# Causal scores in pieces of 64 queries by two experts, and paired half diagonal blocks, in a retention and soft-mixture attention kernel

## The chip, the cores and the metric

The kernel runs on one core of one Trainium2 chip. The metric is the device time of one execution in microseconds (us). TensorE (PE) does the matrix products and transposes, VectorE (DVE), ScalarE (ACT) and GpSimd (POOL) the elementwise work, and SyncE's queue (SP) issues the transfers.

## What is computed

Retention over 8 batches, 8 heads, 576 positions and head size 64 gives `x` of shape (8, 576, 512). On it works causal attention of four experts with head size 64, of which each token weighs the best two. All is float32.

```python
ret = scale * (q @ k.T) * Dmat            # Dmat: gamma ** (i - j) for i >= j, else 0
x = (ret @ v), heads joined               # 8 x 576 x 512
logits = x @ w_gate; best 2 of 4, softmax over them -> w
for e in range(4):
    q, k, v = x @ wq[e], x @ wk[e], x @ wv[e]
    scores = where(causal, -1e9, scale * (q @ k.T))
    a = softmax(scores)
    out += w[e] * ((a @ v) @ wo[e])
```

## The kernel before

Each batch has five chunks of queries, t = 0 to 4: four of 128 and a last one of 64. The 40 chunks go through a pipeline by steps `n`. A step does the retention of chunk `n` (`qk` L135, `old` L164, `own` L174, `st` L115), the attention scores of chunk `n - 6` (`scores`), the transposes of the chunk before it (`turn`), a piece of projections (`work`: q and k in `proj` L225, v in `vproj` L249, output in `outproj` L425), and last the product with the values of the chunk that was transposed (`values`, L400). The order on PE, DVE, ACT and POOL is the order in which the code records the instructions. So each engine works off its own list strictly in that order, and a step is named here by the chunk t whose scores it computes. A table `STEPS` says which piece of projections falls into which step; `end()` writes out the last steps by hand.

All PSUM tiles take turns on eight banks; a new tile waits until the tile eight before it has been read.

Scores (L315, L324): queries and keys of experts 2p and 2p + 1 lie in partitions 0 to 63 and 64 to 127 of pair tile p (index z says which half). Every product has 64 rows and 64 columns of the array. For t < 4 the 128 queries come in two halves i, each against all `w` = t0 + 128 keys. The loops p, i, z let four products in a row use four different quarters of the array. For t = 4 there are 64 queries and 576 keys in two parts j of 288, and output half and row half are both z:

```python
j = i ^ z
mm(ps[p][j][HALF[z]], q[p][HALF[z], l0:l0 + C], k[p][HALF[z], 288 * j:288 * j + 288], ...
```

A float32 product is two instructions on PE, and each has its own weight load.

The softmax takes each expert's scores with one DVE operation that adds the causal mask, negates and takes the extreme (L334; L338 for t = 4), and one ACT exponential with a running sum (L342). `normal` (L354 to L363) scales each expert's row by one over its sum times the gate weight, on DVE. `turn` (L378) transposes each expert's blocks of 128 keys on PE against the identity, up to four blocks in a bank, copied out by ACT (L383) for even experts and by DVE (L381) for odd ones. `values` multiplies with `vn` (L400): the two experts z of a pair stand in the two column halves of the array, all 128 keys of a block in its rows. The last block of t = 4 has only 64 keys and so 64 rows. `gate` (L276 to L292) makes the gate weights on DVE, after `vproj` of a range of chunks has copied out the logits (L254, L256).

Of the kernel before, what the change touches and what calls it, by code (L numbers as in the profile page):

```python
# [33 lines left out]
def kernel(ctx: ExitStack, tc: tile.TileContext, xf, xt, vkf, vkt,  # L34
# [200 lines left out]
    def vproj(b, r, t):  # L235
# [5 lines left out]
        if ti == 0:  # L241
            VN[b, r] = (sb.tile([128, nt, E * D], F32, name=f"vn{r}", bufs=2 - r),
                        sb.tile([128, nt, E], F32, name="lg", tag="lg"))
# [9 lines left out]
        act(vn[:C, ti], ps[:C, :E * D], AF.Copy)  # L253
# [14 lines left out]
    def gate(b, r):  # L268
# [22 lines left out]
        WT[b, r] = wt = sb.tile(sh2, F32, name="wt", tag="wt")  # L291
        v.tensor_mul(wt, ex, mx[:, 2].unsqueeze(2).to_broadcast(sh2))  # L292
# [5 lines left out]
    def scores(m):  # L298
# [6 lines left out]
        n = E if t < 4 else 2  # L305
        if t < 4:
            if t < 2:
                two = [bank([128, 2, w], "ss") for z in range(2)]
                ps = [two[e % 2][:, e // 2] for e in range(E)]
            else:  # L310
                ps = [bank([128, w], "ss") for e in range(E)]
            for p in range(2):
                for i in range(2):
                    for z in range(2):
                        mm(ps[2 * p + z][HALF[i]], q[p][HALF[z], l0 + 64 * i:l0 + 64 * i + 64], k[p][HALF[z], :w],  # L315
                           start=True, stop=True)
        else:
            ps = []
            for p in range(2):
                ps.append([bank([128, 288], "ss") for j in range(2)])  # L320
                for i in range(2):
                    for z in range(2):
                        j = i ^ z
                        mm(ps[p][j][HALF[z]], q[p][HALF[z], l0:l0 + C], k[p][HALF[z], 288 * j:288 * j + 288],  # L324
                           start=True, stop=True)
        p32 = sb.tile([128, n, w], F32, name="p32", tag="p32", bufs=2)
        sm = sb.tile([128, 2, E], F32, name="sm", tag="sm", bufs=3)
        nm = sb.tile([128, E], F32, name="nm", tag="nm", bufs=3)
        SS[m] = (p32, sm, n)

        def soft():
            for e in range(n):
                if t < 4:
                    v.tensor_tensor_reduce(p32[:, e], ps[e], mask[:, 512 - w:], -1.0, BIG, OP.add, OP.min, nm[:, e:e + 1])  # L334
                    bias = nm[:, e:e + 1]
                else:
                    for j in range(2):
                        v.tensor_tensor_reduce(p32[:, e, 288 * j:288 * j + 288], ps[e][j], mask4 if j else mask[:, :288],  # L338
# [3 lines left out]
                act(p32[:, e], p32[:, e], AF.Exp, bias=bias, scale=-1.0, accum_out=sm[:, 0, e:e + 1])  # L342
# [4 lines left out]
    def normal(m):  # L347
# [3 lines left out]
        p32, sm, n = SS[m]  # L351
# [4 lines left out]
        if t < 4:  # L356
            v.tensor_mul(rs, rs, wt[:, ti])
        else:
            for z in range(2):
                hr = slice(64 * z, 64 * z + 64)  # L360
                v.tensor_mul(rs[hr], rs[hr], wt[hr, ti, z::2])
        for e in range(n):
            v.tensor_scalar(p32[:, e], p32[:, e], rs[:, e:e + 1], None, op0=OP.mult)  # L363

    def turn(m):
        b, t = divmod(m, 5)
        p32, sm, n = SS.pop(m)
        nj = t + 1
        pth = sb.tile([128, n, nj, 128], F32, name="pth", tag="pth", bufs=2)
        PT[m] = pth  # L370
        for e in range(n):
            for j0 in range(0, nj, 4):
                js = range(j0, min(nj, j0 + 4))
                rows = slice(0, CH[js[0]][1])
                pt = bank([128, len(js), 128], "pt")
                for j in js:
                    c0, jw = CH[j]
                    nc.tensor.transpose(pt[rows, j - j0], p32[:, e, c0:c0 + jw], ident)  # L378
                o = pth[rows, e, j0:j0 + len(js)]
                if e % 2:  # L380
                    v.tensor_copy(o, pt[rows])  # L381
                else:
                    act(o, pt[rows], AF.Copy)  # L383
# [216 lines left out]
```

## Time and profile before

| what | value |
|---|---|
| median of 3 runs | 473.6 us (473.42 to 474.67) |
| span of the profiled execution | 471.3 us |
| PE busy | 453.0 us (96%) |
| PE weight loads busy | 400.0 us (85%) |
| DVE busy | 323.5 us (69%) |
| ACT busy | 259.5 us (55%) |
| POOL busy | 216.1 us (46%) |
| DMA | 50.98 MB, mean 108 GB/s |

The span goes from the first to the last instruction of the execution that was profiled; the page gives no other time of it, and the median is 2.3 us above the span. Busy times overlap between engines, and a float32 product counts as two instructions. A row of the timeline or of the groups counts a matmul until its result has landed, so that the last instruction of a row adds a fixed tail; differences between rows are free of it.

### The profile page before, as it was taken

How to read it: one execution, taken by the hardware profiler on the slowest of the kernel's cores; microseconds unless marked ns; L12 is line 12 of the kernel's file. 1: busy time of each engine (PE TensorE's matmuls, PEld its weight loads, DVE VectorE, ACT ScalarE, POOL GpSimd, SP SyncE). 2: the span in 40 equal slices, each digit the busy share in tenths (PEclk: the TensorE clock that was granted, in tenths of full speed). 3: DMA queues.
4: the chain of work that ended last, by engine and by line, in shares of the span. 5: the costliest groups of instructions: out<-in, count | busy, mean ns of one | idle time of the engine just before them, and what ended most of it. 6: DMA issues, size and time to landing. Idle time of an engine off the chain costs nothing.

```text
span 471.3 us, 19018 instructions
## 1 busy us (share of the span) xinstructions
PE 453.0 (96%) x7996; PEld 400.0 (85%) x7996; DVE 323.5 (69%) x1136; ACT 259.5 (55%) x814; POOL 216.1 (46%) x275
## 2 busy tenths in 40 slices
PE   7497999999999999999999999999999999999996
PEld 4496988899889898899988998899888998778885
DVE  2735788766797668976687658975679656882662
ACT  2653666555666456645564555654565555663472
POOL 1437464544564454654455445654546544511100
PEclk9589999999999999999999999999999999999999
DMA  7946223314261233314233143512423110010022
GB/s 288 381 142 219 91 93 116 113 46 147 92 217 56 84 134 110 137 47 144 96 131 108 39 143 106 210 50 92 146 92 136 48 58 3 2 47 1 2 79 78
DMA packets 22516, 50.98 MB, mean 108 GB/s; under 512 B 2720, under 2 KB 11680, under 8 KB 22432
## 3 DMA queue, kind: packets, MB, share of 16 engines
q1 hardware_dynamic: 22432, 49.77, 30.4%
q8 instruction: 63, 1.03, 1.0%
q14 instruction: 21, 0.17, 0.1%
HBM read 40.33 MB, written 9.44 MB: 106 GB/s over the span
## 4 chain that ended last, share of the span: by engine, by line
PE 89%; ACT 3%; DVE 3%; POOL 2%; DMA 2%; issue 1%; SPq 0%; ACTq 0%; POOLq 0%; DVEq 0%
PE pj L225 22%; PE ys L400 11%; PE po L425 11%; PE pv L249 11%; PE pt L378 10%; PE ss L315 8%; PE qk L135 4%; PE ss L324 3%; PE own L174 3%; PE st L115 3%; PE old L164 3%; DMA gi<-gi 2%; POOL x L184 1%; ACT gi L101 1%; DVE p L363 1%
## 5 line engine op out<-in xcount | busy, mean ns | idle before, releaser
L342 ACT ACTIVATE p<-p,nm 128x128 f32<-128x128 f32 (+4 forms) x144 | 83.1, 578 | 79.1 <-DVE nm L334 57.6
L186 POOL TENSOR_TENSOR xl<-x,xh 128x512 fp32r<-128x512 f32 (+1 forms) x38 | 45.3, 1192 | 96.5 <-ACT xh L185 96.5
L363 DVE TENSOR_SCALAR p<-p,sm 128x128 f32<-128x128 f32 (+4 forms) x144 | 78.7, 607 | 1.4
L414 POOL CAST yh<-y 128x256 fp32r<-128x256 f32 (+1 forms) x39 | 16.5, 424 | 113.6 <-ACT y L413 113.6
L334 DVE CUSTOM_DVE_ANT_0 p<-ss,mask 128x512 f32<-128x512 f32 (+3 forms) x128 | 56.4, 483 | 8.3 <-PE ss L315 7.9
L179 DVE TENSOR_TENSOR x<-x,own 128x256 f32<-128x256 f32 (+1 forms) x80 | 26.4, 364 | 51.2 <-ACT x L167 49.7
L378 PEld LDWEIGHTS pt<-con,p 128*128 128x128 f32 (+1 forms) x400 | 42.9, 139 | 20.2 <-issue 12.1
L141 POOL TENSOR_SCALAR_AFFINE_SELECT p<-p 64x512 f32<-64x512 f32 (+1 forms) x80 | 48.9, 611 | 23.3 <-ACT p L138 20.5
L400 PE MATMUL ys<-pth,vn 128*64 128x128 f32 (+2 forms) x960 | 56.6, 262 | 0.0
L378 PE MATMUL pt<-con,p 128*128 128x128 f32 (+1 forms) x400 | 52.9, 278 | 1.3 <-DVE nm L334 1.1
L400 PEld LDWEIGHTS ys<-pth,vn 128*64 128x64 f32 (+1 forms) x960 | 46.2, 136 | 8.1 <-issue 3.1
L184 POOL TENSOR_TENSOR x<-x,gi 128x512 f32<-128x512 f32 (+1 forms) x38 | 44.8, 1178 | 3.8 <-DVE x L179 0.5
L315 PE MATMUL ss<-k,q 64*64 64x512 f32 (+3 forms) x512 | 42.6, 432 | 0.0
L381 DVE COPY pth<-pt 128x512 f32<-128x512 f32 (+3 forms) x80 | 37.9, 485 | 4.8 <-PE pt L378 4.4
L102 POOL TENSOR_TENSOR vk<-vk,con 128x512 f32<-128x512 f32 (+1 forms) x34 | 33.9, 997 | 0.0
L383 ACT ACTIVATE pth<-pt 128x512 f32<-128x512 f32 (+3 forms) x80 | 33.1, 419 | 0.5 <-PE pt L378 0.4
L413 ACT ACTIVATE y<-ys 128x256 f32<-128x256 f32 (+1 forms) x39 | 14.1, 362 | 32.7 <-PE ys L400 32.3
L138 ACT ACTIVATE p<-qk 128x256 f32<-128x256 f32 (+1 forms) x80 | 24.6, 360 | 11.2 <-PE qk L135 11.2
L185 ACT ACTIVATE xh<-x 128x512 fp32r<-128x512 f32 (+1 forms) x40 | 23.2, 580 | 11.4 <-POOL x L184 7.2
L425 PE MATMUL po<-yh,who 128*128 128x320 f32 (+1 forms) x128 | 28.8, 306 | 0.6 <-ACT yh L409 0.6
L253 ACT ACTIVATE vn<-pv 128x256 f32<-128x256 f32 (+1 forms) x40 | 15.0, 380 | 24.9 <-PE pv L249 24.9
L225 PE MATMUL pj<-xh,whk 128*128 128x320 f32 (+1 forms) x128 | 24.2, 313 | 4.5 <-ACT xh L185 4.2
(89 smaller groups left out, 1022.6 us busy)
## 6 DMA issues: line engine op xcount, KB each, us to landing
x<-xf SPq DMA_DIRECT2D x32, 512.0 KB, 4.2
vk<-vkf SPq DMA_DIRECT2D x32, 512.0 KB, 5.3
out<-ot SPq DMA_DIRECT2D x32, 160.0 KB, 1.9
out<-ot SPq DMA_DIRECT2D x32, 128.0 KB, 1.8
raw<-wraw SPq DMA_DIRECT2D x4, 512.0 KB, 7.6
x<-xt SPq DMA_DIRECT2D x8, 256.0 KB, 2.7
vk<-vkt SPq DMA_DIRECT2D x8, 256.0 KB, 3.2
gi<-gi SPq DMA_DIRECT2D x1, 256.0 KB, 7.6
```

Source lines behind the costliest of these rows:

```text
L141: gp.affine_select(w, w, pattern=[[0, 4 * k], [1, 64]], base=0, channel_multiplier=-1, compare_op=OP.is_ge, fill=0.0)
L184: e.tensor_mul(x32, x32, gi[:, :, t0:t0 + C])
L186: e.tensor_sub(xl[:, :, l0:l0 + C], x32, f(xh[:, :, l0:l0 + C]))
L225: mm(ps, ww[:, kc, p * 128:(p + 1) * 128], xx[:, kc], start=(i == 0), stop=(i == 11))
L249: mm(ps[:C], xx[:, kc, l0:l0 + C], ww[:, kc], start=(i == 0), stop=(i == 11))
L315: mm(ps[2 * p + z][HALF[i]], q[p][HALF[z], l0 + 64 * i:l0 + 64 * i + 64], k[p][HALF[z], :w], start=True, stop=True)
L334: v.tensor_tensor_reduce(p32[:, e], ps[e], mask[:, 512 - w:], -1.0, BIG, OP.add, OP.min, nm[:, e:e + 1])
L342: act(p32[:, e], p32[:, e], AF.Exp, bias=bias, scale=-1.0, accum_out=sm[:, 0, e:e + 1])
L363: v.tensor_scalar(p32[:, e], p32[:, e], rs[:, e:e + 1], None, op0=OP.mult)
L378: nc.tensor.transpose(pt[rows, j - j0], p32[:, e, c0:c0 + jw], ident)
L400: mm(py[64 * z:64 * z + 64, p], VN[b, rr][0][jr, j - 2 * rr, e * D:(e + 1) * D], src, start=(j == 0), stop=(j == t))
L425: mm(ps, ww[:, p, d * 128:(d + 1) * 128], yy[:, p], start=(i == 0), stop=(i == 5))
```

## The change

For t < 4 a score piece now holds one half s of the chunk's queries (64) for the two experts z of each pair p: output half is p, tile is (s, z), and the first half ends at its own last key t0 + 64. `n` tiles e = 2s + z replace the four experts. For t = 4 the output half is p as well, and j is the outer loop. The mask is one triangle of 64 by 64 for all. The sums, weights and scalings follow this layout: `gate` writes its weights in four pieces (s, p), and `normal` puts the 64 diagonal keys of tile 1 behind those of tile 0. So one block of 128 holds the diagonal keys of the first query half for two experts z, and one transpose takes it. `turn` lists all blocks and puts four into a bank; ACT and DVE copy banks in turn. `values` reads the blocks of both query halves for j < t as one moving operand of two runs of 64, the full diagonal block of the second half by itself, and the paired diagonal block against `vd`, which holds the values of the chunk's first 64 keys for expert z in rows 64z to 64z + 63 and zeros in the other half. `vproj` writes `vd` with one more ACT and one more DVE copy, and the kernel clears it once at its start on POOL.

```diff
-    mask4 = const.tile([128, 288], F32, name="mask4")
-    gp.memset(mask[:, :384], 0.0)
-    gp.memset(mask4[:, :224], 0.0)
+    gp.memset(mask[:, :448], 0.0)
+    vd = [const.tile([128, 2, 2, D], F32, name=f"vd{t}") for t in range(5)]
+    for t in range(5):
+        for z in range(2):
+            gp.memset(vd[t][64 * (1 - z):64 * (1 - z) + 64, z], 0.0)
...
-        act(vn[:C, ti], ps[:C, :E * D], AF.Copy)
+        half = ps[:64, :E * D].rearrange("k (p z d) -> k p z d", p=2, z=2)
+        if t < 4:
+            act(vn[:, ti], ps[:, :E * D], AF.Copy)
+        act(vd[t][:64, 0], half[:, :, 0], AF.Copy)
+        v.tensor_copy(vd[t][64:, 1], half[:, :, 1])
...
-        v.tensor_mul(wt, ex, mx[:, 2].unsqueeze(2).to_broadcast(sh2))
+        for s in range(2):
+            ns = 2 if s else nt
+            for p in range(2):
+                v.tensor_mul(wt[HALF[p], :ns, s], ex[HALF[s], :ns, 2 * p:2 * p + 2],
+                             mx[HALF[s], 2, :ns].unsqueeze(2).to_broadcast([64, ns, 2]))
...
-            for p in range(2):
-                for i in range(2):
+            for s in range(2):
+                for p in range(2):
                     for z in range(2):
-                        mm(ps[2 * p + z][HALF[i]], q[p][HALF[z], l0 + 64 * i:l0 + 64 * i + 64], k[p][HALF[z], :w],
+                        e = 2 * s + z
+                        mm(ps[e][HALF[p]], q[p][HALF[z], l0 + 64 * s:l0 + 64 * s + 64], k[p][HALF[z], :ws[e]],
                            start=True, stop=True)
         else:
-            ps = []
-            for p in range(2):
-                ps.append([bank([128, 288], "ss") for j in range(2)])
-                for i in range(2):
+            ps = [[bank([128, 288], "ss") for j in range(2)] for z in range(2)]
+            for j in range(2):
+                for p in range(2):
                     for z in range(2):
-                        j = i ^ z
-                        mm(ps[p][j][HALF[z]], q[p][HALF[z], l0:l0 + C], k[p][HALF[z], 288 * j:288 * j + 288],
+                        mm(ps[z][j][HALF[p]], q[p][HALF[z], l0:l0 + C], k[p][HALF[z], 288 * j:288 * j + 288],
...
         for e in range(n):
-            v.tensor_scalar(p32[:, e], p32[:, e], rs[:, e:e + 1], None, op0=OP.mult)
+            parts = [(e, 0, ws[e])] if e != 1 else [(1, 0, t0)] * (t > 0) + [(0, t0 + 64, 64)]
+            for f_, c0, cw in parts:
+                i0 = c0 if f_ == e else t0
+                v.tensor_scalar(p32[:, f_, c0:c0 + cw], p32[:, e, i0:i0 + cw], rs[:, e:e + 1], None, op0=OP.mult)
...
+        blocks = [p32[:, z, 128 * j:128 * j + 128] for z in range(2) for j in range(t)] + [p32[:, 0, t0:t0 + 128]]
+        if t < 4:
+            blocks += [p32[:, 2 + z, 128 * j:128 * j + 128] for z in range(2) for j in range(t + 1)]
...
+            for j in range(t):
+                for z in range(2):
+                    a0 = z * t + j
+                    st = 2 * t + 1 + z
+                    src = pth[:, a0:a0 + st + 1:st, h] if t < 4 else pth[:, a0, h]
+                    e = 2 * p + z
+                    mm(py[HALF[z], p], VN[b, j // 2][0][:, j % 2, e * D:(e + 1) * D], src, start=(j == 0), stop=False)
+            if t < 4:
                 for z in range(2):
                     e = 2 * p + z
-                    src = pth[jr, e, j] if t < 4 else pth[jr, p, j, 64 * z:64 * z + 64]
-                    mm(py[64 * z:64 * z + 64, p], VN[b, rr][0][jr, j - 2 * rr, e * D:(e + 1) * D], src,
-                       start=(j == 0), stop=(j == t))
+                    mm(py[HALF[z], p, 64:], VN[b, r][0][:, t % 2, e * D:(e + 1) * D],
+                       pth[:, 2 * t + 1 + z * (t + 1) + t, h], start=(t == 0), stop=(t == 0))
+            for z in range(2):
+                mm(py[HALF[z], p, :64], vd[t][:, z, p], pth[:, 2 * t, h], start=(t == 0), stop=True)
```

Three places show how instructions move; a product is one row here. First, PE, scores of the first t = 4 chunk, before (`ss_1603` to `ss_1610` are the four banks, `k0` and `k1` the pairs p):

```order
L324 MATMUL ss_1603<-k0_381,q01_863 64x288
L324 MATMUL ss_1604<-k0_381,q01_863 64x288 x2
L324 MATMUL ss_1603<-k0_381,q01_863 64x288
L324 MATMUL ss_1609<-k1_382,q11_864 64x288
L324 MATMUL ss_1610<-k1_382,q11_864 64x288 x2
L324 MATMUL ss_1609<-k1_382,q11_864 64x288
```

and with the change:

```order
L334 MATMUL ss_1629<-k0_392,q01_881 64x288
L334 MATMUL ss_1631<-k0_392,q01_881 64x288
L334 MATMUL ss_1629<-k1_393,q11_882 64x288
L334 MATMUL ss_1631<-k1_393,q11_882 64x288
L334 MATMUL ss_1630<-k0_392,q01_881 64x288
L334 MATMUL ss_1632<-k0_392,q01_881 64x288
L334 MATMUL ss_1630<-k1_393,q11_882 64x288
L334 MATMUL ss_1632<-k1_393,q11_882 64x288
```

There are eight products as before, but four in a row now have four different pairs of row half (z, by bank) and column half (p).

Second, PE, the values of a t = 4 chunk, before (`vn_609` and `vn_1058` are the values of chunks 0 and 1 and of chunks 2 to 4):

```order
L400 MATMUL ys<-pth,vn_609 64x64 x4
L400 MATMUL ys<-pth,vn_1058 64x64 x6
L400 MATMUL ys<-pth,vn_609 64x64 x4
L400 MATMUL ys<-pth,vn_1058 64x64 x6
L135 MATMUL qk<-x 64x64 x16
```

and with the change, behind the values of t = 1 (its rows 1 to 6 took the place of eight products `ys<-pth,vn_609 64x128`):

```order
L411 MATMUL ys<-pth,vn_620 64x128 x2
L415 MATMUL ys<-pth,vn_620 64x64 x2
L418 MATMUL ys<-pth,vd_77 64x64 x2
L411 MATMUL ys<-pth,vn_620 64x128 x2
L415 MATMUL ys<-pth,vn_620 64x64 x2
L418 MATMUL ys<-pth,vd_77 64x64 x2
```

```order
L411 MATMUL ys<-pth,vn_620 64x64 x4
L411 MATMUL ys<-pth,vn_1070 64x64 x4
L418 MATMUL ys<-pth,vd_80 64x64 x2
L411 MATMUL ys<-pth,vn_620 64x64 x4
L411 MATMUL ys<-pth,vn_1070 64x64 x4
L418 MATMUL ys<-pth,vd_80 64x64 x2
```

The number of products is the same for t = 4, and all of them now have 128 rows; for t < 4 a pair of 128 columns became two pairs of 64.

Third, DVE, the end of the step of t = 1, before (`p` is the tile of scores, `sm` the sums, `lg` the logits):

```order
L357 TENSOR_TENSOR sm<-sm,wt 128x4
L363 TENSOR_SCALAR p_2054<-p_2054,sm 128x256 x4
L254 COPY lg<-pv 128x4 x2
L254 COPY lg<-pv 64x4
L256 COPY lg<-pv 64x4
```

and with the change:

```order
L368 TENSOR_TENSOR sm<-sm,wt 128x4
L373 TENSOR_SCALAR p_2087<-p_2087,sm 128x192
L373 TENSOR_SCALAR p_2087<-p_2087,sm 128x128
L373 TENSOR_SCALAR p_2087<-p_2087,sm 128x64
L373 TENSOR_SCALAR p_2087<-p_2087,sm 128x256 x2
L259 COPY vd_78<-pv 64x128
L260 COPY lg<-pv 128x4
L259 COPY vd_79<-pv 64x128
L260 COPY lg<-pv 128x4
L259 COPY vd_80<-pv 64x128
L260 COPY lg<-pv 64x4
L262 COPY lg<-pv 64x4
```

There are five scalings in the place of four, and a copy into `vd` ahead of each copy of logits.

## Rows read from the trace of the kernel before

**Rows 1.** The page: busy time by engine, and the ending chain by engine.
```profile
PE 453.0 (96%) x7996; PEld 400.0 (85%) x7996; DVE 323.5 (69%) x1136; ACT 259.5 (55%) x814; POOL 216.1 (46%) x275
...
PE 89%; ACT 3%; DVE 3%; POOL 2%; DMA 2%; issue 1%; SPq 0%; ACTq 0%; POOLq 0%; DVEq 0%
```
**Rows 2.** Busy time by stretch, start and one batch: length, busy us per engine, granted clock.
```profile
0.00:45.00 45.00, 32.66 (x818) 27.12 (x820) 19.50 (x53) 20.03 (x58) 19.64 (x28) 0.85 0.73 264
...
173.50:228.00 54.50, 54.50 (x1007) 49.04 (x1001) 39.86 (x140) 31.20 (x99) 27.96 (x36) 1.00 0.32 111
```
**Rows 3.** Groups by shape, PE, scores: busy us, mean ns, idle before.
```profile
L324 PE MATMUL ss<-k,q 64*64 64x288 f32 x128 | 17.5, 404 | 0.0
L315 PE MATMUL ss<-k,q 64*64 64x512 f32 x128 | 15.6, 591 | 0.0
...
L315 PE MATMUL ss<-k,q 64*64 64x384 f32 x128 | 12.7, 485 | 0.0
...
L315 PE MATMUL ss<-k,q 64*64 64x256 f32 x128 | 9.1, 379 | 0.0
...
L315 PE MATMUL ss<-k,q 64*64 64x128 f32 x128 | 5.2, 273 | 0.0
```
**Rows 4.** Timeline, PE, transposes of t = 1 and t = 2: start, us.
```profile
174.88 1.09 PE L378 MATMUL pt<-con,p 128*128 128x128 f32 x8
...
185.77 1.53 PE L378 MATMUL pt<-con,p 128*128 128x128 f32 x12
```
**Rows 5.** Timeline, PE, values of t = 1 and t = 2.
```profile
181.66 1.09 PE L400 MATMUL ys<-pth,vn 128*64 128x128 f32 x16
...
190.07 1.53 PE L400 MATMUL ys<-pth,vn 128*64 128x128 f32 x24
```
**Rows 6.** Timeline, PE, values of t = 4, windows of 0.3 and 0.6 us.
```profile
212.34 0.45 PE L400 MATMUL ys<-pth,vn 128*64 128x64 f32 x8
...
212.34 0.69 PE L400 MATMUL ys<-pth,vn 128*64 128x64 f32 x16
```
**Rows 7.** Chain, values of t = 4 and t = 0 up to the next `old`.
```profile
212.41 1.70 PE ys L400 x38
...
214.63 0.47 PE old L164 x31
...
225.53 0.59 PE ys L400 x8
...
226.74 0.47 PE old L164 x32
```
**Rows 8.** Timeline, from the scalings of t = 3 to its values.
```profile
189.74 3.63 DVE L363 TENSOR_SCALAR p<-p,sm 128x512 f32<-128x512 f32 x4
...
193.12 2.12 PE L324 MATMUL ss<-k,q 64*64 64x288 f32 x16
...
198.09 0.58 ACT L383 ACTIVATE pth<-pt 128x512 f32<-128x512 f32 x1
...
199.93 0.88 PE L400 MATMUL ys<-pth,vn 128*64 128x128 f32 x12
```
**Rows 9.** Groups by shape, DVE: a scaling, a small copy, the gate product.
```profile
L363 DVE TENSOR_SCALAR p<-p,sm 128x128 f32<-128x128 f32 x32 | 7.1, 286 | 0.3
...
L381 DVE COPY pth<-pt 64x128 f32<-64x128 f32 x8 | 2.2, 273 | 0.0
...
L292 DVE TENSOR_TENSOR wt<-ex,mx 128x12 f32<-128x12 f32 x8 | 1.4, 172 | 0.3
```
**Rows 10.** Timeline of the last steps.
```profile
445.88 1.67 DVE L363 TENSOR_SCALAR p<-p,sm 128x512 f32<-128x512 f32 x4
...
448.37 0.49 PE L378 MATMUL pt<-con,p 128*128 128x128 f32 x3
...
458.33 0.88 DVE L381 COPY pth<-pt 128x512 f32<-128x512 f32 x2 [3.81 <-PE pt L378]
458.44 1.82 PE L400 MATMUL ys<-pth,vn 128*64 128x64 f32 x40
```

More of the change, by code (lines that the diff above doesn't have):

```diff
@@ L350, in normal @@
         ti = t - RNG[r][2][0]
[L351 removed]
+        t0 = CH[t][0]
+        p32, sm, n, ws = SS[m]
         wt = WT[b, r]
@@ L355, in normal @@
         v.reciprocal(rs, sm[:, 0, :n])
[L356 to L361, printed above, removed]
+        v.tensor_mul(rs, rs, wt[:, ti].rearrange("p s z -> p (s z)") if t < 4 else wt[:, ti, 0])
         for e in range(n):
-            v.tensor_scalar(p32[:, e], p32[:, e], rs[:, e:e + 1], None, op0=OP.mult)
+            parts = [(e, 0, ws[e])] if e != 1 else [(1, 0, t0)] * (t > 0) + [(0, t0 + 64, 64)]
+            for f_, c0, cw in parts:
+                i0 = c0 if f_ == e else t0
+                v.tensor_scalar(p32[:, f_, c0:c0 + cw], p32[:, e, i0:i0 + cw], rs[:, e:e + 1], None, op0=OP.mult)
     def turn(m):
         b, t = divmod(m, 5)
-        p32, sm, n = SS.pop(m)
-        nj = t + 1
-        pth = sb.tile([128, n, nj, 128], F32, name="pth", tag="pth", bufs=2)
-        PT[m] = pth
[L371 to L383, printed above, removed]
-                yield
+        t0 = CH[t][0]
+        p32 = SS.pop(m)[0]
+        blocks = [p32[:, z, 128 * j:128 * j + 128] for z in range(2) for j in range(t)] + [p32[:, 0, t0:t0 + 128]]
+        if t < 4:
+            blocks += [p32[:, 2 + z, 128 * j:128 * j + 128] for z in range(2) for j in range(t + 1)]
+        pth = sb.tile([128, len(blocks), 128], F32, name="pth", tag="pth", bufs=2)
+        PT[m] = pth
+        for n, i0 in enumerate(range(0, len(blocks), 4)):
+            js = blocks[i0:i0 + 4]
+            pt = bank([128, len(js), 128], "pt")
+            for i, src in enumerate(js):
+                nc.tensor.transpose(pt[:, i], src, ident)
+            o = pth[:, i0:i0 + len(js)]
+            if n % 2:
+                v.tensor_copy(o, pt)
+            else:
+                act(o, pt, AF.Copy)
+            yield
     def values(m):
@@ L506 @@
             nc.sync.dma_start(rg, wraw[:, 4096:].rearrange("p (k w) -> p k w", k=4))
-            nc.sync.dma_start(mask[:, 384:], con_d[:, 220:])
-            for z in range(2):
-                nc.sync.dma_start(mask4[64 * z:64 * z + 64, 224:], con_d[:64, 220:284])
+            nc.sync.dma_start(mask[:, 448:], con_d[:, 220:])
         if n in (1, 4):
@@ L578, in _tables @@
     con[:, 200:220] = np.repeat(fac, 64, axis=0)
-    con[:, 220:348] = np.triu(np.full((128, 128), -1e9), 1)
+    con[:, 220:284] = np.tile(np.triu(np.full((64, 64), -1e9), 1), (2, 1))
     e = np.arange(E)
```

26 lines of the change are left out of this document (13 added, 13 removed).

## The prediction

> **What bounds the kernel now.** I read the page first. PE is busy 96% of the span, and the chain of work that ended last is 89% PE [rows 1], while DVE, the next, has 69%. Such shares are means, so I went on to the busy time by stretch: in one batch in the middle (54.5 us) PE is busy all of it, DVE 39.86 us, ACT 31.20 us, POOL 27.96 us, at full granted clock [rows 2]. PE works off its list without a gap there. So what PE's list loses in the six middle batches comes off the time, as long as the data that PE waits for come as much sooner. The first 45 us are another matter (PE busy 32.66 us, clock 0.85), but the change has no score piece in them, so I count nothing there. Then I took PE's groups by shape and its timeline for the price of each edit, and the rows of DVE and ACT around the one step where their work comes just in time.
>
> **The sum, on PE.** All times are set against the span of 471.3 us. The median is 473.6 us, 2.3 above it; I take that as what lies around the span and leave it.
>
> Scores of t = 4. Eight tiles, one a batch, took 17.5 us [rows 3], 2.19 us each. Before, only two quarters of the array are used (row half and column half are both z); now four are, as in the products of t < 4. Those cost 9.1 / 8 = 1.14 us for 256 keys and 12.7 / 8 = 1.59 us for 384 with the same eight products, so 288 keys come to 1.14 + 0.45 x 32/128 = 1.25 us. That saves 0.94 us a batch, 7.5 us in all.
>
> Scores of t < 4. From 128 to 512 keys the tile goes from 5.2 / 8 = 0.65 to 15.6 / 8 = 1.95 us [rows 3], 1.30 us for 384 columns in all eight products. Four of the eight lose 64 columns: 1.30 x 64/384 x 1/2 = 0.108 us, 32 times, 3.5 us.
>
> Transposes. Each tile has one less (4, 8, 12, 16, 10 become 3, 7, 11, 15, 9), 40 in all. Four more cost 1.53 - 1.09 = 0.44 us [rows 4], 0.11 us each: 4.4 us saved.
>
> Values of t < 4. Eight more instructions with 128 columns cost 0.44 us [rows 5], so a pair of experts (four instructions) 0.22 us. With 64 columns eight cost 0.69 - 0.45 = 0.24 us [rows 6], a pair 0.12 us. For each tile and p one pair at 0.22 becomes two at 0.12: +0.02, 64 times, 1.3 us more.
>
> Values of t = 4. The pairs with only 64 rows go. From the last end before the values to the start of the next `old` the chain has 214.63 - 212.41 = 2.22 us; for t = 0, where all pairs have 128 rows, 226.74 - 225.53 = 1.21 us with two pairs of 0.22 [rows 7]. Ten pairs of 0.12 in their place make 1.21 - 0.44 + 1.20 = 1.97 us. That saves 0.25 us, 2.0 us in all.
>
> Sum: -7.5 - 3.5 - 4.4 + 1.3 - 2.0 = -16.1 us.
>
> **What is given back.** DVE gets more instructions. Each batch has five copies into `vd` (0.27 us by the nearest copy), four more scalings (0.29 us for the nearest, 128 wide) and six more gate products (0.17 us) [rows 9]: at most 3.5 us, without the score and copy columns that fall away. That makes 43.4 us at most in a batch of 52.5 us, no new bound on the whole. ACT's five copies into `vd`, of which one takes the place of `vn`'s, have the idle 23 us of its batch. The ten clearings on POOL come ahead of its first selection, which waits for the first products of the retention; were they not covered there, they would delay only the first chunk. The mask's one transfer in the place of three frees SP; nothing on the path waits for it.
>
> The place to watch is the step of t = 4. The values of t = 3 start at 199.93, and the last ACT copy of their blocks ends at 198.09 + 0.58 = 198.67 [rows 8]: 1.26 us to spare. PE gains ahead of it, since the scores of t = 3: 0.11 there, 0.11 in the transposes of t = 2, 0.94 in the scores of t = 4 and 0.11 in those transposes, less 0.04 in the values of t = 2: 1.23 us. The copy is at the end of a chain on DVE and ACT that PE's gain does not pull forward: the four scalings of t = 3 take 3.63 us, 0.9 each for 512 columns [rows 8], though the four in the last steps take 1.67 us [rows 10]; POOL works beside the former. Five scalings of 1920 columns in all stand in place of four of 2048. The fifth costs between nothing (fewer columns make up for it) and 0.9 us (a slow one). I take 0.15 us a batch, near the lower end because 128 columns fewer save 0.2 us at that rate; over seven batches 1.0 us.
>
> The last steps give back more. Before the transposes of the last t = 3 tile the scalings end at 445.88 + 1.67 = 447.55, and PE starts at 448.37 [rows 10], 0.82 us to spare. Those scalings wait for the gate, which now has a copy into `vd` (0.27) and three more products (0.5) ahead of it, and for one more scaling. So the 0.94 us that PE gains in the scores just before is waited out: 0.9 us back. For the last t = 4 tile the values now need both experts' banks at once; before, the first matmul started at 458.44 while DVE's copies went on until 459.21 [rows 10], 0.77 us later. A transpose less and one copy fewer soften this: 0.5 us back.
>
> -16.1 + 1.0 + 1.4 = -13.7 us: 473.6 - 13.7 = **459.9 us**, or a span of 457.6.
>
> **The rivals.**
>
> *The step of t = 4 turns to DVE's bound.* If each fifth scaling costs 0.9 us, the slow rate above, all of it lies on PE from the second batch on, for there is no room left (1.26 against 1.23). In place of 0.15 us that is 0.9 us a batch, 5.3 us more: 465.2 us. For it: the slow rate is there in this very step, four times in a row. Against: the columns get fewer. Chance 0.14.
>
> *The change doesn't do what it says for t = 4:* four quarters don't run beside each other there. Then 7.5 us of the sum are gone: 467.4 us. Against: the products of t < 4 have the same four quarters in the same order and run at 1.14 us for 256 keys. Chance 0.04.
>
> *Weight loads show.* The new products in `values` are short, and each instruction brings a load of 64 columns. If these loads did not hide, the 256 added instructions (960 become 1216) would cost half a transpose with its load of 128 columns each, 0.055 us: 14.1 us, 474.0 us, no change. The row speaks against it: with 64 columns eight instructions take 0.24 us [rows 6], 0.03 each, less than 0.055, so their loads already run beside the products. The Trainium skill, "TensorE: Matmul & The Clock Gate", Part 3 under "What overlaps and what doesn't", says that a weight load runs beside a matmul in flight only where the row groups differ, and in `values` all products use all rows; by that rule this rival would be the likeliest. The trace disagrees with it, as the 0.24 us show. Chance 0.03.
>
> *Slower: the moving operand in two runs.* For j < t the values read two blocks of 64 columns that lie apart, by one instruction. No row shows that shape; the nearest are single runs of 64 and 128 columns, 0.12 and 0.22 us a pair [rows 5, 6]. Below, it costs nothing; above, if each run were read as long as a full one, 0.22 us more for each of 12 pairs a batch, 2.64 us, 21.1 us in all: 481.0 us. It decides from 13.7 / 96 = 0.14 us a pair. I take nothing, since the columns are the same. Chance 0.03.
>
> **How the numbers follow.** The forecast with its own spread (give-backs of 0 to 5 us) has 0.76, the rivals 0.14, 0.04, 0.03 and 0.03. Nothing given back makes 457.5; a little below that, for price rows that round, is the lower end, 456.8. The upper end takes in most of DVE's rival: 465.0. About 0.15 is left out. A measurement of this kernel can tell about 0.3%, 1.4 us, from no change. Faster by over that: the forecast and the first two rivals, 0.94; within it, the weight loads, 0.03; slower, the two runs, 0.03.
>
> **What would show it.** Right: on PE, t = 4 scores fall from 2.19 to about 1.25 us a tile with the same instruction count, 360 transposes stay, 64-column pairs in `values` stay at 0.12 us, and a middle batch takes 52.5 to 53 us. DVE's rival: idle time ahead of the values of t = 3, with ACT's or DVE's copy of the blocks as the releaser. Two runs: `values` rows of t = 1 to 3 that grow by more than 0.04 us a tile. Weight loads: pairs of 64 columns well over 0.12 us. The last steps: a wait ahead of the transposes of the last t = 3 tile, with DVE's scalings as the releaser. Wrong altogether would be a middle batch of 54 us or more with no group of PE's longer: then a wait that I have not seen took the gain.

## The result and the profile after

| | before | after |
|---|---|---|
| median | 473.51 us (472.54 to 474.67, 4 runs) | 468.81 us (467.65 to 469.49, 4 runs) |
| ratio | | 0.9899 [0.9878, 0.992] |
| span of the profiled execution | 471.3 us | 467.1 us |

The change gains 4.7 us where 13.7 were forecast, and the time lies above the range's upper end of 465.0. The page of the changed kernel, first the busy times, then the ending chain, then the queue that carries PE's instructions (number of packets, MB, share of 16 engines); the first two answer to [rows 1]:

```profile
PE 445.1 (95%) x8212; PEld 397.8 (85%) x8212; DVE 335.7 (72%) x1208; ACT 260.8 (56%) x830; POOL 219.5 (47%) x284
...
q8 instruction: 65, 1.06, 0.9%
...
PE 73%; DVE 12%; ACT 9%; issue 2%; DMA 2%; POOL 1%; SPq 0%; DVEq 0%; ACTq 0%; POOLq 0%
```

PE's busy time fell by 7.9 us, the span by 4.2 alone. The chain says where to look: DVE and ACT, 3% each before, now hold 21% of it. The groups by shape on PE (busy us, mean ns, idle before), to be laid beside [rows 3]:

```profile
L388 PE MATMUL pt<-con,p 128*128 128x128 f32 x360 | 48.7, 279 | 1.5 <-DVE nm L349 1.1 <-DVE p L373 0.2
L411 PE MATMUL ys<-pth,vn 128*64 128x128 f32 x384 | 33.4, 280 | 1.6 <-ACT pth L393 1.6
...
L334 PE MATMUL ss<-k,q 64*64 64x288 f32 x128 | 10.0, 406 | 0.7 <-DVE lg L260 0.7
```

The t = 4 scores went from 17.5 to 10.0 us, 1.25 a tile, just as forecast. But they now have 0.7 us of idle time before them, and the values 1.6 us, with ACT's copies of the blocks as the releaser. Where PE stands still is told by the busy time by stretch. I divided both traces where the first projection product of a t = 0 or t = 2 step starts. Before (length, busy us of PE, PEld, DVE, ACT, POOL, granted clock, DMA share, GB/s):

```profile
45.20:65.90 20.70, 20.29 (x395) 18.29 (x392) 17.07 (x68) 11.77 (x39) 12.49 (x14) 1.00 0.30 95
...
175.70:230.30 54.60, 54.60 (x1002) 49.10 (x1000) 39.89 (x141) 31.20 (x100) 28.06 (x36) 1.00 0.32 110
...
424.80:471.30 46.50, 42.49 (x410) 35.78 (x410) 21.23 (x78) 20.98 (x61) 4.82 (x10) 1.00 0.12 41
```

and after:

```profile
45.70:69.40 23.70, 21.70 (x401) 18.88 (x399) 19.34 (x75) 12.67 (x44) 12.44 (x14) 0.93 0.33 105
...
176.90:230.10 53.20, 53.00 (x1027) 48.49 (x1026) 41.45 (x150) 31.19 (x102) 28.31 (x36) 1.00 0.33 113
...
420.30:467.10 46.80, 40.99 (x440) 34.97 (x439) 22.64 (x90) 22.62 (x66) 5.32 (x11) 1.00 0.13 46
```

With the dividing points to the hundredth, the differences are:

| stretch | before | after | difference |
|---|---|---|---|
| to the first batch's t = 0 projections | 45.21 | 45.67 | +0.46 |
| on to its t = 2 projections | 20.71 | 23.70 | +2.99 |
| six batches, to the last one's t = 2 | 327.99 | 322.25 | -5.74 |
| on to its t = 0 (the last steps' order) | 30.93 | 28.65 | -2.28 |
| on to the end | 46.45 | 46.80 | +0.35 |

The forecast's 1.86 us a batch (16.1 / 8 less 0.15) would be -11.2 for the six batches. So two things have to be explained: 5.4 us in the six batches, and 3 us lost at once in the first batch, where I had looked for no loss (by the sum that stretch should have won 0.4 us). The start's 0.46 us is less than the changed kernel's runs below differ there among themselves (44.34 to 46.30), and the last two stretches come to 1.9 us where the forecast has 2.1.

**The first batch.** Timeline of the changed kernel from the t = 1 scalings (start, us):

```profile
59.79 3.63 DVE L373 TENSOR_SCALAR p<-p,sm 128x192 f32<-128x192 f32 x5
...
63.44 0.28 DVE L259 COPY vd<-pv 64x128 f32<-64x128 f32 x1
63.73 0.16 DVE L260 COPY lg<-pv 128x4 f32<-128x4 f32 x1
...
64.04 0.33 PE L176 MATMUL own<-p,vk 64*64 64x64 f32 x4 [1.77 <-POOL p L143]
...
64.53 0.68 PE L176 MATMUL own<-p,vk 64*64 64x64 f32 x28 [0.16 <-DVE lg L260]
...
66.17 2.55 PE L327 MATMUL ss<-k,q 64*64 64x320 f32 x16
```

The same place before:

```profile
59.29 3.10 DVE L363 TENSOR_SCALAR p<-p,sm 128x256 f32<-128x256 f32 x4
...
62.31 0.28 DVE L254 COPY lg<-pv 128x4 f32<-128x4 f32 x3
...
62.60 0.75 PE L174 MATMUL own<-p,vk 64*64 64x64 f32 x30 [0.41 <-DVE lg L254]
```

The `own` products need a bank that holds value projections (`pv`), and DVE frees it by its copies, which stand behind the scalings of t = 1. Before, three copies of logits took 0.28 us together; now a `vd` copy goes ahead of each, and the scalings are five. PE stands for 1.77 us instead of 0.41. (The row names POOL's selection as releaser. It isn't that: in a run below the same products start before it. PE goes on 0.15 us after the first `lg` copy, 63.73 + 0.16 us, and stands again until the second.) Other batches have the output projections in this step as cover, the first has none yet. In this execution, behind the wait, the granted clock falls to the lower of its two levels, 1.2 GHz; windows of 1 us of the changed kernel:

```profile
63.00:64.00 1.00, 0.00 (x0) 0.00 (x0) 0.94 (x4) 0.06 (x1) 0.94 (x2) 1.00 0.62 127
...
66.00:67.00 1.00, 1.00 (x24) 0.72 (x23) 0.57 (x4) 0.00 (x0) 0.80 (x1) 0.50 0.71 139
67.00:68.00 1.00, 1.00 (x12) 0.27 (x4) 0.79 (x5) 0.00 (x0) 0.46 (x1) 0.50 0.94 356
```

PE did nothing from 63 to 64; from 66 to 68 the clock is 0.50.

**The step of t = 4.** Timeline after, the rows that answer to [rows 8]:

```profile
190.81 4.21 DVE L373 TENSOR_SCALAR p<-p,sm 128x448 f32<-128x448 f32 x5
...
194.10 1.15 PE L334 MATMUL ss<-k,q 64*64 64x288 f32 x16
...
199.90 0.58 ACT L393 ACTIVATE pth<-pt 128x512 f32<-128x512 f32 x1
...
199.93 0.43 PE L411 MATMUL ys<-pth,vn 128*64 128x128 f32 x2
...
200.53 0.76 PE L411 MATMUL ys<-pth,vn 128*64 128x128 f32 x9 [0.17 <-ACT pth L393]
```

Before, the last ACT copy ended 198.67 - 189.74 = 8.93 us after the start of the t = 3 scalings; now 200.48 - 190.81 = 9.67. Of the 0.74 us more, the scalings are 0.58 (4.21 against 3.63). PE starts the values of t = 3, does two instructions, and stands until 200.53. They take 2.53 us up to the next `qk` where they took 1.90.

**The last steps.** Timeline after, to be laid beside [rows 10]:

```profile
441.23 1.74 DVE L373 TENSOR_SCALAR p<-p,sm 128x448 f32<-128x448 f32 x5
...
443.40 2.27 PE L388 MATMUL pt<-con,p 128*128 128x128 f32 x15 [1.09 <-DVE nm L349]
...
454.50 0.62 PE L411 MATMUL ys<-pth,vn 128*64 128x64 f32 x13 [0.21 <-DVE pth L391]
...
457.77 0.68 PE L411 MATMUL ys<-pth,vn 128*64 128x128 f32 x8 [0.55 <-ACT pth L393]
```

### The profile page after: what moved, and what is told of

It is laid out like the page before. It is cut to its first block, busy times and chain, and to the rows that moved or that the text cites. A ratio compares the mean times of both kernels' runs of the same rounds, so it can differ in the third digit from the quotient of the medians.

```text
span 467.1 us, 19651 instructions
## 1 busy us (share of the span) xinstructions
PE 445.1 (95%) x8212; PEld 397.8 (85%) x8212; DVE 335.7 (72%) x1208; ACT 260.8 (56%) x830; POOL 219.5 (47%) x284
## 3 DMA queue, kind: packets, MB, share of 16 engines
q8 instruction: 65, 1.06, 0.9%
## 4 chain that ended last, share of the span: by engine, by line
PE 73%; DVE 12%; ACT 9%; issue 2%; DMA 2%; POOL 1%; SPq 0%; DVEq 0%; ACTq 0%; POOLq 0%
PE pj L227 22%; PE po L442 10%; PE pv L251 7%; PE ss L327 7%; PE ys L411 7%; PE pt L388 6%; PE qk L137 4%; PE own L176 3%; DVE p L349 3%; DVE p L373 2%; PE st L117 2%; PE old L166 2%; ACT p L353 2%; PE ys L418 2%; DMA gi<-gi 2%
## 5 line engine op out<-in xcount | busy, mean ns | idle before, releaser
L353 ACT ACTIVATE p<-p,nm 128x64 f32<-128x64 f32 (+6 forms) x144 | 79.6, 554 | 86.0 <-DVE nm L344 57.8
L373 DVE TENSOR_SCALAR p<-p,sm 128x64 f32<-128x64 f32 (+8 forms) x176 | 88.3, 566 | 1.4
L388 PEld LDWEIGHTS pt<-con,p 128*128 128x128 f32 x360 | 38.7, 141 | 21.5 <-issue 10.2
L344 DVE CUSTOM_DVE_ANT_0 p<-ss,mask 128x128 f32<-128x128 f32 (+7 forms) x128 | 52.3, 452 | 6.2 <-PE ss L327 6.1
L388 PE MATMUL pt<-con,p 128*128 128x128 f32 x360 | 48.7, 279 | 1.5 <-DVE nm L349 1.1
L411 PE MATMUL ys<-pth,vn 128*64 128x128 f32 (+1 forms) x640 | 43.9, 258 | 1.9 <-ACT pth L393 1.6
L327 PE MATMUL ss<-k,q 64*64 64x448 f32 (+7 forms) x512 | 42.1, 416 | 0.6 <-issue 0.6
L411 PEld LDWEIGHTS ys<-pth,vn 128*64 128x64 f32 x640 | 31.3, 137 | 8.5 <-ACT pth L393 3.6
L393 ACT ACTIVATE pth<-pt 128x512 f32<-128x512 f32 (+1 forms) x64 | 32.6, 514 | 0.6 <-PE pt L388 0.3
L176 PE MATMUL own<-p,vk 64*64 64x64 f32 x1152 | 28.9, 226 | 3.3 <-POOL p L143 1.8
L187 ACT ACTIVATE xh<-x 128x512 fp32r<-128x512 f32 (+1 forms) x40 | 23.1, 578 | 11.2 <-POOL x L186 7.1
```

Of the source, the lines that this page charges most:

```text
L176: mm(own[r][HALF[u], g, i], vk[HALF[r], s, 0, 2 * g + u], p[HALF[r], g, s, u], start=True, stop=True)
L327: mm(ps[e][HALF[p]], q[p][HALF[z], l0 + 64 * s:l0 + 64 * s + 64], k[p][HALF[z], :ws[e]], start=True, stop=True)
L344: v.tensor_tensor_reduce(p32[:, e, :ws[e]], ps[e], mask[:, 512 - ws[e]:], -1.0, BIG, OP.add, OP.min, nm[:, e:e + 1])
L353: act(p32[:, e, :ws[e]], p32[:, e, :ws[e]], AF.Exp, bias=bias, scale=-1.0, accum_out=sm[:, 0, e:e + 1])
L373: v.tensor_scalar(p32[:, f_, c0:c0 + cw], p32[:, e, i0:i0 + cw], rs[:, e:e + 1], None, op0=OP.mult)
L388: nc.tensor.transpose(pt[:, i], src, ident)
```

## The experiments

Theory A was that PE's gain is real and is waited out behind DVE: at the values of t = 3 in every batch, and at the banks in the first.

**One part undone: the quarters.** The t = 4 scores in an order that names only two quarters of the array in its first four products and the other two in the rest:

```diff
-            for j in range(2):
-                for p in range(2):
-                    for z in range(2):
+            for d in range(2):
+                for j in range(2):
+                    for z in range(2):
+                        p = z ^ d
```

> Edit: the changed kernel with the t = 4 score products recorded so that only two quarters of the array lie side by side (z, then p = z xor d), eight products as before. Theory A (the gain of the t = 4 scores is mostly waited out, since the values of t = 3 wait for a chain on DVE and ACT): the t = 4 scores go from 1.25 back to about 2.2 us a tile by the rows, PE's list grows by 0.9 us a batch, but the wait of 0.6 us ahead of the values of t = 3 goes; net +0.3 us a batch in seven, so about 470 to 472 us against 468.8. Rival B (that wait has nothing to do with the scores' gain, each microsecond on PE's list counts): +0.9 a batch, 7 us in all, about 476 us.

468.45 us, ratio 0.9907 [0.9888, 0.9927]. The edit did not do what it was made for. The group of the scores:

```profile
L335 PE MATMUL ss<-k,q 64*64 64x288 f32 x128 | 11.6, 410 | 0.7 <-DVE lg L260 0.7
```

11.6 us instead of 10.0, far from the 17.5 of two quarters [rows 3], so it says nothing about A or B.

**The scores twice.** A cleaner way to take PE's gain back: the same products, issued once more.

```diff
-            for j in range(2):
+            for j in [0, 1, 0, 1]:
```

> The changed kernel with every score product of the t=4 step issued twice into the same banks (the same products, so nothing is left out). It puts back about 1.05 us of TensorE work a batch where the change took 0.9 us out. Theory A (most of what the scores gave there is waited out later in the same step, at the t=3 values, behind the fifth scaling and ScalarE's copy): the wait of 0.57 us there shrinks to nothing, so the time rises by the rest alone, 0.4 to 0.6 us a batch, 3 to 5 us in all: 472 to 474 us. Rival B (TensorE bounds the step from end to end, and the missing gain lies elsewhere): the whole 1.05 us a batch shows, 8 to 9 us in all: 477 to 478 us, and the t=3 values still wait.

471.67 us, ratio 0.9961 [0.9946, 0.9976], 2.9 us above the change. Its timeline:

```profile
192.54 2.12 PE L334 MATMUL ss<-k,q 64*64 64x288 f32 x32
...
199.25 0.88 PE L411 MATMUL ys<-pth,vn 128*64 128x128 f32 x12
```

The scores have grown by 2.12 - 1.15 = 0.97 us, and the values run without a stand. A middle batch takes 53.6 us, against 53.2 with the change. So of 0.97 us a batch 0.4 shows; the rest had been waited out. This decides for A in its place, the step of t = 4. The median is a little under A's 472 to 474; the first batch's clock stays full in this trace (more of that below).

**One scaling fewer on DVE.** For t = 3 the two halves of the diagonal block are brought together by products with the identity, not by a fifth scaling:

```diff
-            parts = [(e, 0, ws[e])] if e != 1 else ...
+            parts = [(e, 0, ws[e])] if e != 1 or t == 3 else ...
...
+                if src is None:
+                    for z in range(2):
+                        mm(pt[HALF[z], i], p32[:, z, t0:t0 + 64], ident, start=True, stop=True)
```

> Edit: the changed kernel; for t = 3 alone the scaling of tile 1 is one instruction again, the diagonal keys stay where they are, and two float32 products against the identity (one per column half, two instructions each) put their transposes into the paired block. PE's list grows by about 0.11 us a batch, DVE's chain of t = 3 loses the fifth scaling. Theory A: the scalings of t = 3 end about 0.5 us sooner after their start, the wait ahead of the values of t = 3 falls from about 0.6 to 0.1 us, net -0.4 us a batch, about 466 us. Rival B (the fifth scaling is hidden; the wait is ACT's own order of copies): the wait stays, +0.1 us a batch, about 469.5 us.

468.16 us, 0.9893 [0.9873, 0.9913]: the change's time, where A had about 466 us. The four scalings take 3.57 us and the stand at the values is gone (1.93 us), as A had it, but with these products the transposes took 2.02 us instead of 1.61, 0.41 more where I had counted 0.11. What was won on one side was mostly paid on the other: a middle batch takes 53.0 us.

**The last scaling of t = 3 on ACT.**

```diff
+                if t == 3 and e == 3:
+                    act(p32[:, f_, c0:c0 + cw], p32[:, e, i0:i0 + cw], AF.Copy, scale=rs[:, e:e + 1])
+                    continue
```

> Edit: the changed kernel with the scaling of tile 3 of t = 3 on ACT in place of DVE. It takes about 0.9 us of DVE's chain of t = 3 and puts 0.7 us on ACT. Theory A: the t = 4 softmax begins up to 0.9 us sooner, no wait is left ahead of the values of t = 3, 0.6 us a batch less: about 465 us. Rival B (ACT is the one that is late there): the wait stays or grows, 469 to 472 us.

464.59 us, 0.9817 [0.9797, 0.9837], 4.2 us below the change. Its timeline:

```profile
190.38 3.35 DVE L376 TENSOR_SCALAR p<-p,sm 128x448 f32<-128x448 f32 x4
...
198.82 0.59 ACT L396 ACTIVATE pth<-pt 128x512 f32<-128x512 f32 x1
...
199.41 0.93 PE L414 MATMUL ys<-pth,vn 128*64 128x128 f32 x12
```

The copy ends at 198.82 + 0.59 = 199.41, just when PE comes to the values: no stand, 1.97 us for them. A middle batch takes 52.6 us. This is Theory A's time, and near the 52.5 us that PE's sum alone gives (54.55 before, less 2.01).

**The second `vd` copy on ACT.**

```diff
-        v.tensor_copy(vd[t][64:, 1], half[:, :, 1])
+        act(vd[t][64:, 1], half[:, :, 1], AF.Copy)
```

> Edit: the changed kernel with the second copy into vd on ACT too, none on DVE. Theory A for the first batch: the products own behind its t = 1 step wait for the banks of the value projection, which DVE frees behind five slow scalings and three copies into vd; without the copies they start 0.6 to 0.9 us sooner, and the granted clock may or may not fall behind that shorter gap: -0.7 us without, -2.2 us with the clock kept, 466.5 to 468 us; the wait ahead of the values of t = 3 stays at 0.6 us, since the copies stand behind that chain. Rival B (the copies cost nothing): 468.8 us.

466.62 us, 0.9867 [0.985, 0.9884]. In the step of t = 2 the `own` products fell from 0.64 to 0.47 us, their time before. But in that of t = 4 they rose in four of the six batches, from 0.35 to 0.63 and more, and a middle batch still takes 53.25 us: the wait only moved. Of the 1.6 us that its span is shorter, 1.33 lie ahead of the first batch's t = 0 projections, where the traces differ by nearly 2 us (44.34 to 46.30) without a reason in the kernels.

**PE kept busy in the first batch.**

```diff
+        if n == 7:
+            for i in range(12):
+                mm(old[0], wz, wz[:, None, :].to_broadcast([128, 2, 128]), start=True, stop=True)
```

> The changed kernel with twelve short bf16 products of zeros (256 columns each) into a bank that is about to be overwritten, put once, in the first batch's t=2 step, where TensorE otherwise waits. Theory A (the half clock of 65 to 68 us follows from the idle time of TensorE before it, and costs about 1.5 us): the granted clock stays at 1.0 there, and the time falls by 1 to 1.7 us: 467 to 468 us. Rival B (the low clock doesn't hang on that idle time, or these products cost what they save): the same stretch still shows 0.5, and the time is 469 to 470 us.

467.97 us, 0.9883 [0.9864, 0.9902]. The same two windows:

```profile
66.00:67.00 1.00, 1.00 (x40) 0.75 (x35) 1.00 (x5) 0.00 (x0) 0.39 (x1) 1.00 1.01 389
67.00:68.00 1.00, 1.00 (x12) 0.48 (x5) 1.00 (x5) 0.25 (x1) 0.88 (x1) 1.00 0.57 184
```

The clock stays at 1.00, as Theory A had it. The stretch to the t = 2 projections takes 22.15 us instead of 23.70, 1.55 less; the medians differ by 0.84. The wait itself stays. But this run does not show that the products kept the clock. In the runs with two quarters and with the scores twice, which are the change's code up to this point, PE stands there just as long (1.74 and 1.73 us; 1.74 in the change), and the clock stays at 1.00 too. The second window, in the run with two quarters:

```profile
67.00:68.00 1.00, 1.00 (x13) 0.52 (x6) 1.00 (x5) 0.28 (x1) 0.84 (x1) 1.00 0.83 287
```

The stretch takes 22.17 and 22.15 us in these two. In seven of the fourteen traces of this study PE stands there for 1.7 to 2.2 us, and the clock falls behind it in five; in the other seven it stands for 0.6 us or less, and the clock falls in none. So idle time of PE goes ahead of the fall, which costs about 1.5 us where it comes; what else decides it stays open.

**The first batch's copies on ACT.** All seven DVE copies out of the value banks for t = 2 to 4 of that batch:

```diff
+        early = b == 0 and r == 1
+        copy = (lambda o, i: act(o, i, AF.Copy)) if early else v.tensor_copy
```

> The changed kernel with the seven copies out of the value products' banks that VectorE makes for t=2 to 4 of the first batch given to ScalarE (the second half-block copies and the gate logits'); all other batches are as in the change. Theory A (in the first batch's t=1 step TensorE waits some 1.5 us for a bank that these copies free only behind five scalings on VectorE, and the half clock after it costs about as much again): the own products start some 1.5 us sooner, and the time falls by 1.5 to 3 us, to 466 to 467.5 us. Rival B (the wait there hides under others, on ScalarE's copies or the loads): within 0.5 us of the change, 468.3 to 469.3 us.

465.30 us, 0.9836 [0.9811, 0.9862], 3.5 us below the change. Its timeline:

```profile
59.58 3.02 DVE L375 TENSOR_SCALAR p<-p,sm 128x192 f32<-128x192 f32 x5
...
61.68 0.34 ACT L260 ACTIVATE lg<-pv 64x4 f32<-64x4 f32 x2
...
61.89 0.65 PE L176 MATMUL own<-p,vk 64*64 64x64 f32 x31
```

ACT has freed the banks while the scalings still run, `own` starts 2.15 us sooner, and the t = 2 projections start at 65.11 where the change has 69.37. The trace gives 1.8 us of it back in the batch that follows. So the wait in the first batch is shown to come from DVE's copies behind its scalings; the low clock came on top of it in the profiled execution of the change.

**The reliefs together.** Both moves to ACT (the `vd` copy for t < 4 alone), then with the twelve short products, then with the first batch's copies instead of these:

> The changed kernel with two things moved from VectorE to ScalarE: the scaling of the t=3 step's last tile, and the second copy into the half-empty value blocks for t below 4. Theory A (VectorE's chain in the t=4 step, 0.5 to 0.65 us a batch, and its wait for banks in the t=2 step, 0.15 us a batch, are two separate losses): both go, and the time is that of the scaling alone less 1 to 2 us: 462.5 to 463.5 us. Rival B (ScalarE now takes over the same waits): no better than the scaling alone, 464.5 us or more.

> The two moves to ScalarE and the twelve short products of the first batch together. Theory A: the three losses add, and the time is 461 to 462 us, the granted clock 1.0 in the first batch's t=2 step. Rival B (the low clock moves elsewhere or the products cost what they save): the same as with the two moves alone, within 0.5 us.

> The two moves to ScalarE of all batches (the scaling of the t=3 step's last tile, and the second half-block copy for t below 4) together with the first batch's copies on ScalarE, without the short products. Theory A: the wait for banks in the first batch goes as well, 1 to 1.5 us below the two moves alone, 460.7 to 461.3 us. Rival B: the same as with the two moves alone, within 0.5 us of 462.2 us.

462.20 us, 0.9772 [0.9749, 0.9795]; 462.06 us, 0.9758 [0.9739, 0.9777]; 463.18 us, 0.9774 [0.9752, 0.9797]. The two moves add up, 2.4 us under the scaling alone. The short products add nothing that can be measured. The last is a miss: it should have come to 461. Its first batch is 3.2 us shorter than that of the two moves alone (20.47 us to the t = 2 projections instead of 23.67), but the t = 4 step after it gives 1.2 back, as it does in the run before. There the values of t = 2, sooner now, wait for ACT's copies, and take 2.27 us instead of 1.49; `own` takes 0.76 instead of 0.36:

```profile
80.63 0.43 PE L419 MATMUL ys<-pth,vn 128*64 128x128 f32 x2
...
81.41 0.54 PE L419 MATMUL ys<-pth,vn 128*64 128x128 f32 x5 [0.35 <-ACT pth L401]
```

The profiled spans are 461.5 us for it and 462.9 for the two moves alone, the other way round than the medians, and the runs of the one spread over 2.0 us, of the other over 2.8; so nothing is shown between the two. The second of the three, 462.06 us, is the best time of this study.

**The stands that nothing releases.** Three of the changed kernel's batches are longer than 53.2 us by 0.6 to 1.1 us, each with one stand at the scores of t = 1 or t = 2 or just ahead of them. One of these stands:

```profile
322.93 0.32 PEld L327 LDWEIGHTS ss<-k,q 64*64 64x64 f32 x6
...
324.07 0.19 PEld L327 LDWEIGHTS ss<-k,q 64*64 64x64 f32 x2 [0.82 <-issue]
324.07 0.64 PE L327 MATMUL ss<-k,q 64*64 64x256 f32 x2 [0.36 <-issue]
```

I counted all of PE's instructions by their start, from zero: the loads and products, 2 x 8212 = 16,424, and the 349 that stand between them, nearly all waits for semaphores, 16,773 together. The three stands end at numbers 4,545, 12,481 and 14,529, each 193 past a multiple of 256; so does the one of the kernel before (6,081). And the queue of kind instruction has 65 packets of 1.06 MB for them: 63 bytes each, 258 to a packet; the kernel before has 63 packets for 16,284. The Trainium skill, "Perfetto Trace Analysis", under "The 4-stage abstract model", gives an instruction 64 bytes. The row agrees. The three stands also end 2.4 to 2.5 us after a packet of this queue starts (at 119.18, 321.56 and 374.96 us). So these stands lie where PE goes over to the next packet of instructions. To test it, the kernel before got 40 and 128 more tiny products at its start, 80 and 256 instructions:

```diff
-    warm(12)
+    warm(10)
+    pw = bank([128, 512], "pw")
+    for i in range(42):
+        mm(pw[:, :16], wz, wz[:, :16], start=True, stop=True)
```

> The kernel before, with two of its twelve starting products of zeros replaced by 42 tiny ones (16 columns), so that 40 more products, 80 more TensorE instructions, stand ahead of the first batch and nothing else differs. Theory C (TensorE's instructions come in blocks of 256 by the queue of kind instruction; where 256 of them are used up in under about 3 us, the next block is late, and TensorE stands still at the border of the block; the change lost 1.1 us more than the kernel before by this, since its borders fall in other places): every border moves by 80 instructions, into the short products of most batches, and the time rises by 4 to 6 us, to 477.5 to 479.5 us, with still stands of 0.4 to 1 us at most batches that nothing in the profile releases. Rival D (those still stands belong to the work in which they fall, or to the load transfers beside them): they don't move with the count of instructions ahead, and the time is that of before, 473 to 474.5 us.

> The control of the run with 40 more products: the kernel before with six of its starting products replaced by 134 tiny ones, so that 128 more products, 256 more TensorE instructions, one whole block, stand ahead. Theory C: the borders fall in the same places of the work as in the kernel before, and the time is that of before within what the start costs, 473 to 475 us. Rival (more products at the start cost time by themselves, by the clock or the queue): the time rises at least as much as with 40 more.

476.73 us, 1.0073 [1.0047, 1.0098], and 474.50 us, 1.0027 [1.0013, 1.0042]. A stand of the first:

```profile
327.58 0.63 PEld L315 LDWEIGHTS ss<-k,q 64*64 64x64 f32 x13 [0.78 <-issue]
327.58 0.87 PE L315 MATMUL ss<-k,q 64*64 64x256 f32 x11 [0.33 <-issue]
```

and of the second:

```profile
108.42 0.20 PEld L315 LDWEIGHTS ss<-k,q 64*64 64x64 f32 x6 [0.97 <-issue]
108.42 0.66 PE L315 MATMUL ss<-k,q 64*64 64x256 f32 x6 [0.51 <-issue]
```

The places move with the count: 10,177, 12,225 and 14,273 in the one, 4,289 and 6,337 in the other, every one again 193 past a multiple of 256. That settles where they come from, against the work or the loads beside them. Their price is not settled. I had expected 4 to 6 us for the one, and for the other no more than the start costs. From the first batch's t = 2 projections to the last one's t = 0 both are longer than before by about as much, 0.9 and 0.7 us (359.82 and 359.66 against 358.92). Of the 3.6 and 1.4 us of the medians, 1.9 and 0.8 us of the traces lie ahead of that. There is a border that I had overlooked: in each of the fourteen traces PE stands at number 449, in the start. The two shifted kernels stand at number 705 as well, where the kernel before does not. The one stand of the kernel before, and the second of the kernel with 128 more:

```profile
15.45 0.82 PE L174 MATMUL own<-p,vk 64*64 64x64 f32 x18 [1.32 <-issue]
...
18.23 0.83 PE L174 MATMUL own<-p,vk 64*64 64x64 f32 x18 [2.37 <-issue]
```

## Why the prediction was wrong

**PE's prices were right, but for two that wait.** Scores of t = 4: 1.25 us a tile, as forecast. The rest is taken from one kind of product to the next, by the medians of the six batches. The scores of t = 1 and 3 fell by 0.11 and 0.10 us (forecast 0.108), the transposes of t = 1 to 4 by 0.11 (0.11), the values of t = 0 to 2 rose by 0.03 (0.04), and those of t = 4 up to the `old` products fell by 0.25 (0.25). So the rivals of the missing quarters, the two runs and the weight loads all fell. The scores of t = 0 and 2 fell by 0.03 and 0.04 alone (0.108); with the second `vd` copy on ACT they fell by 0.09 and 0.10, so they wait for DVE's copies. And some gains were luck, since nothing forecast them: the transposes of t = 0 fell by 0.29, the k or q projections of the t = 2 step by 0.07, the `old` products behind the values of t = 4 by 0.05, 0.30 us a batch more than counted.

(The row against the weight loads was read too quickly. In `values` two column halves work side by side, 0.055 us an instruction of 128 columns where a transpose takes 0.11. So 0.03 us for 64 columns is 0.06 in each half, which does not lie under the 0.055 that it was held against. It still leaves a load no room, since the 64 columns alone are half of 0.11.)

**The step of t = 4 was mis-sized.** The place, the chain and the releaser were named; the term was 0.15 us a batch "near the lower end", on the ground that 128 columns fewer soften it. They didn't: five scalings take 0.58 us more than four, the chain 0.74, and the values 0.63, of which 0.04 was in the sum. That is 0.44 a batch more than counted. The scores of t = 4 up to the transposes, which wait for DVE too (1.18 us, but 1.08 with a scaling on ACT), fell by 0.87 instead of 0.94. Together that is 3.1 us in the six batches. The row that I had beside it, 0.9 us a scaling in this very step [rows 8], spoke for the rival, and the truth lies nearer to that; the sign named for it, a stand ahead of the values of t = 3 with ACT's copy as the releaser, is there. The runs with the scores twice and with a scaling on ACT show it from both sides. That columns do not set the price where DVE is slow is seen in the changed kernel's own groups: a scaling of 192 columns takes 1.23 us in the mean, one of 512 only 0.77:

```profile
L373 DVE TENSOR_SCALAR p<-p,sm 128x512 f32<-128x512 f32 x24 | 17.7, 765 | 0.0
...
L373 DVE TENSOR_SCALAR p<-p,sm 128x192 f32<-128x192 f32 x8 | 9.8, 1230 | 0.3
```

Why the scalings are slow there was not tested; POOL works beside them, but no run took its work away.

**The copies into `vd` were summed, not queued.** "No new bound on the whole" took DVE's copies as busy time of a batch. But each goes ahead of the copy of logits that frees a bank, and both stand behind the scalings. In the step of t = 2 of each batch that costs `own` 0.17 us (0.64 against 0.47), and the scores of t = 0 and 2 another 0.15; about 1.9 us in six batches. In the first batch, whose t = 1 step has no output projections as cover, it costs 3 us in the profiled execution, half of them by the low clock, and about 1.4 where the clock stays full (22.15 us for that stretch, 20.71 before). "I count nothing there" was said of the first 45 us; I then took all that follows as a middle batch.

**Instruction packets were not thought of.** The three stands of the change come to 0.69 + 0.76 + 0.69 us, from start to start over two instructions, against 0.54 for the one of the kernel before, 1.6 us more; in all, what the longer batches have above the usual one comes to 2.2 us more. With 3.1 and 1.9, less 1.8 for the gains that were not forecast, that makes the 5.4 of the six batches.

**The last steps** were named rightly and priced low. From the first of the output products ahead of the last t = 3 transposes up to these PE needs 4.88 us instead of 3.62, 0.48 more in them, 0.07 in the values of t = 4 and 0.37 in the transposes of t = 2: 2.2 us for the 1.4. The first has a wait in it that I had not seen: the new bank must first be read by the softmax of t = 4 (L349), which stands behind the five scalings on DVE. Against it, a wait of the kernel before went that I hadn't counted as a gain, ahead of the last batch's t = 0 projections:

```profile
423.92 0.64 PE L378 MATMUL pt<-con,p 128*128 128x128 f32 x2 [1.09 <-DVE nm L334]
```

## What to carry to other kernels

Where PE is busy all the time and other work comes just in time beside it, ask of each added instruction on another engine not how long it is but which queue it stands in, and which bank or tile behind it PE waits for; price it at the rate of that step's own rows. Look at the first round of a pipeline by itself, since the work that covers a wait in all other rounds may not be there. A gain on the bounding engine can be tested at once by giving it back (the same products twice): what then does not show in the time had been waited out.

## What was not expected of the hardware

PE takes its instructions in packets, 256 to one by the places of the stands, and a few of the borders between them cost 0.3 to 1.3 us (from start to start) where many short products stand together, and 1.5 to 2.8 us in the start; the stand has no releaser but "issue", and some instructions more or fewer at the start move it elsewhere.

The t = 4 scores ran nearly as fast (11.6 against 10.0 us) with an order that should leave two quarters idle for half of the time. Their sixteen instructions start within 0.94 us in one batch, in the kernel before within 1.72. There each quarter starts an instruction every 0.24 us; if the second half had waited for the last start of the first, at 0.75 us, the last start would come at about 1.5 us by my estimate. So I take it that a product whose quarter is free starts ahead of earlier ones whose quarter is not, against what "The kernel before" says of PE's list; that is inferred from the times, no run tested it by itself. The Trainium skill, "TensorE: Matmul & The Clock Gate", Part 3 under "What overlaps and what doesn't", says that products start strictly in order. This row speaks against it.
